# Loading the first MLP weight earlier, routing two steps per call, and turning the last layer's first group in slots 2 and 3

## The chip, the cores and the metric

The kernel runs on one core of a Trainium2 chip. The metric is the time of one execution on the device in microseconds (us), the median of several runs; lower is better. One execution is also recorded by the hardware profiler, and all rows in this document come from such records. Their engines are PE (TensorE matmuls), PEld (TensorE weight loads), DVE (VectorE), ACT (ScalarE), POOL (GpSimd) and SP (the sync engine, which here only issues DMAs; its queue is written SPq).

## The reference

Three layers follow each other: block-causal attention, a mixture of experts with one expert per token, and an MLP. Cut to what is computed:

```python
# attention: q, k, v are (4, 8, 576, 64) float32
scores = where(block_i >= block_j, q @ k.T / 8, -1e9)      # blocks of 64 tokens
attn = exp(scores - max); attn /= sum + 1e-9
x = (attn @ v) as (2304, 512)

# mixture of experts, 8 experts, 512 -> 1024 -> 512
logits = x @ w_gate + modality_bias[modality_id]
e_idx = argmax(logits); gate_w = softmax(logits)[e_idx]
for e in range(8):
    mask = e_idx == e
    out[mask] = gate_w[mask] * (maximum(x[mask] @ w1[e], 0) @ w2[e])

# MLP 512 -> 2048 -> 512; w_in and w_out arrive as float64
h = out @ w_in
g = where(h >= 1, h, where(h <= -1, 0, (h + 1)**2 / 4))
return g @ w_out
```

## The kernel before

The order of the work on each engine is written out by hand: within a stage every engine runs its instructions in the order in which the Python code emits them, and waits at an instruction until its operands and its buffer are there. Nothing overtakes on an engine, and nothing overtakes in SP's queue of DMA issues. A tile with a tag and a number of buffers reuses them in turn; the next user waits until the last reader is done.

The **slots** are the middle stage. Tokens are sorted by expert and cut into slots of 512 tokens; five slots (0 to 4) always run, the last with 384 tokens, and a branch behind them runs more where the routing asks for it. A slot has eight blocks `(s, f)`, one for 128 of the 1024 hidden columns. In a block, `first(s, f)` is 12 matmuls (w1 of the block times the slot's tokens, in three products of high and low parts) into a PSUM tile `h`; ACT makes `hh` of it and DVE `hl` (lines 1088 and 1089). `second` of the block before is 12 matmuls (9 in slot 4) into the accumulators `acc`. The weights come as `raw` tiles from SP (lines 539 and 541, four buffers); ACT makes the high part `wh` (line 1072) two blocks ahead and DVE the low part `wl` (line 1075) one block ahead. In blocks 3 to 6 `turn` transposes 128 tokens of the next slot on PE into a PSUM tile `xt` (line 1065), from which ACT makes `xhi` (line 75) and DVE `xlo` (line 76). That tile has the tag `tr` in the pool `pst`, which holds one buffer. At a slot's end `acc` is copied to `y` (lines 1105 and 1107) and scattered to `y_dram` by DMAs that POOL issues (line 1109).

`between(s, f, at)` is called four times in a block (`at` 0 to 3), and the side work hangs on it:

- The **routing** is a generator (`group`, `other_slots`) of small steps, mostly one to three DVE instructions. A call takes one step where `at` is even and two where it is odd, six in a block. Three of its steps use PE: the ranks `rkp` (lines 647 to 652), the inverse permutation `inv` (lines 696 and 697), and the tables `tabs` (line 912). Each puts its result in a tile of the same tag `tr`. Between the operands of `inv` and `inv` itself stand 12 steps that do nothing.
- **w_in** comes in 16 pieces of 512 KB (`load_wi`). SP issues the DMA of a piece (`wi_raw`, line 964, two buffers); then `cut_f64` lets 2 steps go by and makes float32 of float64: ACT squares (`sqi`, line 952), DVE does four operations (lines 954, 956, 958, 959). Last come the high part on ACT (line 969) and the low part, a subtraction on POOL (line 970). A step is taken in the calls with odd `at`, two in a block, by each of the last three pieces begun. Pieces are begun after the blocks from (2, 1) to (4, 4), 16 in 21 blocks.
- **The last layer's first group**: three tiles of 128 tokens are fetched from `y_dram` (`yr`, line 1016), scaled by the gate on DVE (line 1023) and transposed by `turn_y` (PE line 1031, ACT line 75, DVE line 76). `AHEAD` names the blocks of fetch, scale and turn for each of the three; all are in slot 4.

After slot 4 all engines pass the branch, and the last layer begins with `first` of its group 0 (line 991, `h<-yhi,wi`).

Of the kernel before, what the change touches and what calls it, by code (L numbers as in the profile page):

```python
# [11 lines left out]
F32 = mybir.dt.float32  # L12
# [6 lines left out]
ALU = mybir.AluOpType  # L19
# [17 lines left out]
NF, NF2 = F // P, F2 // P  # L37
# [5 lines left out]
NSTAT = 5  # L43
# [23 lines left out]
NG = G3 // P  # L67


AHEAD = ((4, 1), (4, 3), (4, 4)), ((4, 1), (4, 4), (4, 5)), ((4, 2), (4, 5), (4, 6))  # L70


def split_hi_lo(nc, hi, lo, src):
# [472 lines left out]
class Routing:  # L546
# [222 lines left out]
    def other_slots(self, ps):  # L769

        nc, V, t = self.nc, self.nc.vector, self.t
# [3 lines left out]
        def T(shape, dt, nm):  # L775
            return t.late_pool.tile(shape, dt, name=nm)
# [34 lines left out]
        nc.scalar.activation(ohp, oha, AF.Copy, scale=self.pcol)  # L811
        V.tensor_tensor(ohj, oha, self.tile0.to_broadcast([P, NJ, NS2]), op=ALU.mult)
        yield
        for _ in range(12):
            yield
        yield from self.inverse(ps("inv")[:, :NS2], U * NFIRST, NJ, ohp, ohj)
        yield "rows"
# [38 lines left out]
        more, some, few = T([P, 1, E], F32, "more"), T([P, 1], F32, "some"), T([P, 1], F32, "few")  # L856
# [20 lines left out]
        n, js, parts = NSORT, slice(0, NSORT), 5  # L877
# [18 lines left out]
                        op=ALU.is_equal)  # L896
# [29 lines left out]
def experts_and_mlp(ctx, bctx, late, tc, a_tail, weights, w_in, w_out, x_dram, y_dram, g_dram, out,  # L926
                    ident, half, tabs):
    nc = tc.nc
# [13 lines left out]
    def cut_f64(pool, u, raw, nm, wait, bufs=2):  # L942

        w = raw.bitcast(I32).rearrange("p (f w) -> p f w", w=2)
        top, bot = w[:, :, 1], w[:, :, 0]
        sq = pool.tile([P, 512], F32, tag="sq", name=f"sq{nm}", bufs=bufs)
        ti, ui = sq.bitcast(I32), u.bitcast(I32)


        for _ in range(wait):  # L950
            yield
        nc.scalar.activation(sq, top.bitcast(F32), AF.Square)
        yield
        nc.vector.scalar_tensor_tensor(sq, sq, 2.0 ** -30, top.bitcast(F32), op0=ALU.is_ge, op1=ALU.mult)

        nc.vector.tensor_scalar(ui, ti, 3, 0x3FFFFFFF, op0=ALU.logical_shift_left, op1=ALU.bitwise_and)
        yield
        nc.vector.scalar_tensor_tensor(ui, ti, -0x40000000, ui, op0=ALU.bitwise_and, op1=ALU.bitwise_or)
        nc.vector.scalar_tensor_tensor(ui, bot, 29, ui, op0=ALU.logical_shift_right, op1=ALU.bitwise_or)
        yield  # L960

    def load_wi(g):
        raw = tabs.cv.tile([P, 512], I64, tag="raw64", name=f"wi_raw{g}")
        nc.sync.dma_start(out=raw.rearrange("p (c f) -> p c f", f=P),
                          in_=w_in[:, g * P:(g + 1) * P].rearrange("(c p) f -> p c f", p=P))
        u = tabs.cv.tile([P, 512], F32, tag="cu", name=f"cui{g}", bufs=2)
        yield from cut_f64(tabs.cv, u, raw, f"i{g}", 2)
        hi, lo = (x.rearrange("p c f -> p (c f)") for x in wi[g])
        nc.scalar.copy(hi, u)
        nc.gpsimd.tensor_tensor(lo, u, hi.bitcast(F32), op=ALU.subtract)  # L970

    wo_raw, wo_left = {}, [z + i * NF2 // 2 for z in range(NF2 // 2) for i in range(2)]

# [26 lines left out]
    def open_right():  # L1000
        late.close()
        tabs.cv = pool("cv", 2, bctx)
        right = dict(side="right")
        res = pool("c_w", 1, **right)
        tabs.res = res

        for i, (tag, n, bufs) in enumerate(AREA):
            a = res.tile([P, n, 2, ND, P], F32R, tag=tag, name=f"wi{i}", bufs=bufs)
            wi.extend((a[:, z, 0], a[:, z, 1]) for z in range(n))
        tabs.rows = pool("c_rows", 3, yctx, **right)  # L1010
        y_ps.append(pool("c_y", 1, yctx, **right))
# [23 lines left out]


    def run_slots(slots, begin, between, part=0):
        blocks = [(s, f) for s in slots for f in range(NF)]

# [81 lines left out]
        for z, (s, f) in enumerate(blocks):  # L1121
            nxt = s + 1 if s + 1 in slots else None
            if f == 1 and nxt:
                gather(nxt)
            if z + CONV < len(blocks):
                convert(*blocks[z + CONV], 0)
            between(s, f, 0)
            if z + CONV - 1 < len(blocks):
                convert(*blocks[z + CONV - 1], 1)
            weights.load()  # L1130
            between(s, f, 1)
            if (s, f) == (NSTAT - 1, NF - 2) and not part:
                tc.mark_branch_hint_location("more", engines=ENGINES)

            first(s, f)
            between(s, f, 2)
            if z > 0:
                second(*blocks[z - 1])
            if f in TURNS and nxt:
                turn(nxt, TURNS.index(f))  # L1140
            between(s, f, 3)
# [27 lines left out]
    more = itertools.chain(early, routing.other_slots(lambda nm: pst.tile([P, 512], F32, tag="tr", name=nm)))  # L1169
    begun, conv = [], []  # L1170
    state = dict(more=True, placed=False)

    def between(s, f, at):
        last = at == 3
        if state["more"] and (s or f or last):
            for _ in range(1 + at % 2):
                try:
                    got = next(more)
                    if got == "experts":
                        for x in range(NFIRST, NSTAT):  # L1180
                            weights.know(x)
                            weights.blocks += [(x, f) for f in range(NF)]
                    elif got == "rows":
                        state["placed"] = True
                except StopIteration:
                    state["more"] = False
                    open_right()
                    break
        if at % 2:
            for x in conv:  # L1190
                next(x, None)
        if not last or s == 0:
            return
        assert state["placed"]
        for t, places in enumerate(AHEAD):
            for place, do in zip(places, (fetch, scale, turn_y)):
                if place == (s, f):
                    do(0, t)

        z, n, m = NF * (s - 2) + f + 1, NF2, NF * (NSTAT - 2) - 3  # L1200
        if z > 0 and z * n // m > (z - 1) * n // m and len(begun) < n:
            g = len(begun)
            begun.append(load_wi(g))
            conv[:] = begun[-3:]
# [329 lines left out]
```

## Time and profile before

| | |
|---|---|
| median of 3 runs | 853.55 us (853.25 to 854.59) |
| the profiled execution's own time | 853.72 us |
| its span, first to last instruction | 851.9 us |
| PE busy | 824.9 us (97%) |
| DVE, ACT, POOL busy | 604.9, 480.1, 226.0 us |
| slots 0 to 4 | 222.7 to 455.2 us of the span |

The page divides the span into 40 slices of 21.3 us and gives the busy tenths of each engine:

```
PE   6999999998999999999888999999999999999998
DVE  5778878789755564888774666666635788777774
```

(PE's row is the page's; a slice that reads 8 has up to 4 us without a matmul.) The slices that read 888 in PE's row are 405 to 469 us: slot 4 and the start of the last layer.

### The profile page before, as it was taken

The page shows a single profiled execution, that of the slowest core. Times are in us where ns is not written, and L with a number is a line of the kernel's source. Part 1 is how long each engine was busy: PE and PEld are TensorE (multiplying, and loading weights), DVE is VectorE, ACT ScalarE, POOL GpSimd, SP SyncE. Part 2 cuts the span into 40 slices and gives each one's busy share as a digit, 9 for nine tenths or more (in the row PEclk, how much of TensorE's full clock was granted, in tenths as well). Part 3 has the DMA queues.
Part 4 walks back from the last instruction along what each step waited for, and adds up shares of the span by engine and source line. Part 5 has one row for each costly group of instructions (what it writes and reads, how often), then busy time and mean ns, then how long its engine had stood idle before and what let it go on. Part 6 is the DMA issues. An engine that isn't in the chain of part 4 may idle for free. (4 is left out here: it accounts for less than half of the span.)

```text
span 851.9 us, 14940 instructions
## 1 busy us (share of the span) xinstructions
PE 824.9 (97%) x5430; PEld 738.9 (87%) x5430; DVE 604.9 (71%) x1098; ACT 480.1 (56%) x958; POOL 226.0 (27%) x265
## 2 busy tenths in 40 slices
PE   6999999998999999999888999999999999999998
PEld 5787787785888888888767999999999999999998
DVE  5778878789755564888774666666635788777774
ACT  5898888885534343445434666666656533343431
POOL 8555555556302212242312000110000012111110
PEclk8999999999999999999999999999999999999999
DMA  6343443430924445564642553554633454333301
GB/s 147 73 100 86 105 111 93 112 88 28 293 88 161 149 136 180 173 218 152 208 127 95 166 180 126 173 179 143 210 131 139 140 218 154 124 137 124 124 29 35
DMA packets 137294, 116.16 MB, mean 136 GB/s; under 512 B 69799, under 2 KB 122039, under 8 KB 134912
## 3 DMA queue, kind: packets, MB, share of 16 engines
q1 hardware_dynamic: 131488, 100.90, 38.6%
q0 software_dynamic: 4384, 13.92, 4.6%
q8 instruction: 44, 0.72, 0.4%
q10 hardware_dynamic: 1344, 0.33, 0.2%
q14 instruction: 34, 0.28, 0.1%
HBM read 82.09 MB, written 33.29 MB: 135 GB/s over the span
## 5 line engine op out<-in xcount | busy, mean ns | idle before, releaser
L991 PE MATMUL h<-yhi,wi 128*128 128x384 f32 x768 | 200.4, 338 | 1.1 <-ACTq L1225 1.1
L991 PEld LDWEIGHTS h<-yhi,wi 128*128 128x128 f32 x768 | 139.5, 188 | 1.6 <-ACTq L1225 1.6
L991 PE MATMUL h<-ylo,wi 128*128 128x384 f32 x384 | 129.2, 336 | 0.0
L325 ACT ACTIVATE pall<-s,nmax 128x384 f32<-128x384 f32 (+2 forms) x144 | 79.5, 559 | 26.7 <-DVE nmax L319 17.0
L1264 ACT ACTIVATE cl<-h,half 128x384 f32<-128x384 f32 x96 | 55.8, 581 | 68.5 <-PE h L991 61.2
L1268 DVE SCALAR_TENSOR_TENSOR gg<-cl,h 128x384 f32<-128x384 f32 x96 | 52.1, 551 | 49.0 <-ACT cl L1265 40.0
L1388 PE MATMUL p<-wo,s 128*128 128x256 f32 x648 | 83.6, 282 | 0.4 <-DVE rest L1407 0.4
L1388 PEld LDWEIGHTS p<-wo,s 128*128 128x128 f32 x648 | 80.3, 188 | 0.6 <-issue 0.6
L1432 POOL DMA_INDIRECT out_dram<-rest,tab x16 | 24.7, 1544 | 195.3 <-DVE rest L1415 168.7
L991 PEld LDWEIGHTS h<-ylo,wi 128*128 128x128 f32 x384 | 72.1, 188 | 0.0
L343 PE MATMUL pt<-ident,pall 128*128 128x128 f32 x400 | 64.7, 279 | 3.3 <-DVE pT L484 2.4
L991 PE MATMUL h<-xhi,wl 128*128 128x512 f32 (+2 forms) x164 | 61.9, 378 | 2.0 <-DVE wl L1075 1.9
L991 PE MATMUL h<-xhi,wh 128*128 128x512 f32 (+2 forms) x164 | 63.4, 386 | 0.0
L1100 PE MATMUL acc<-wh,hh 128*128 128x512 f32 x152 | 60.1, 396 | 3.2 <-ACT hh L1088 3.2
L1388 PE MATMUL p<-wo,a 128*128 128x256 f32 x486 | 62.7, 282 | 0.0
L1100 PE MATMUL acc<-wh,hl 128*128 128x512 f32 x152 | 60.1, 395 | 1.7 <-DVE hl L1089 1.7
L991 PE MATMUL h<-xlo,wh 128*128 128x512 f32 (+2 forms) x164 | 61.5, 375 | 0.0
L1388 PEld LDWEIGHTS p<-wo,a 128*128 128x128 f32 x486 | 60.3, 188 | 0.0
L1089 DVE SCALAR_TENSOR_TENSOR hl<-h,hh 128x512 fp32r<-128x512 f32 (+1 forms) x40 | 26.5, 662 | 47.5 <-ACT hh L1088 47.2
L1100 PE MATMUL acc<-wl,hh 128*128 128x512 f32 x152 | 59.7, 393 | 0.0
L368 PE MATMUL px<-pT,v 128*64 128x512 f32 (+4 forms) x320 | 52.4, 432 | 0.0
L1265 ACT ACTIVATE cl<-cl 128x384 f32<-128x384 f32 x96 | 50.5, 526 | 3.0
(314 smaller groups left out, 1830.5 us busy)
## 6 DMA issues: line engine op xcount, KB each, us to landing
raw<-in_moe_w_dram SPq DMA_DIRECT2D x80, 256.0 KB, 3.0
g_dram<-gg SPq DMA_DIRECT2D x48, 384.0 KB, 2.8
g<-g_dram SPq DMA_DIRECT2D x18, 1024.0 KB, 4.8
wi_raw<-in_moe_w_in_dram SPq DMA_DIRECT2D x16, 512.0 KB, 5.2
wo_raw<-in_moe_w_out_dram SPq DMA_DIRECT2D x16, 512.0 KB, 4.2
yr<-y_dram SPq DMA_DIRECT2D x18, 256.0 KB, 3.7
x_dram<-xrow SPq DMA_DIRECT2D x33, 128.0 KB, 1.8
v<-in_v_dram SPq DMA_DIRECT2D x32, 128.0 KB, 2.6
```

The lines of the kernel that those rows point to most:

```text
L325: nc.scalar.activation(pall[n % 2][:, o:o + w], pss[:, u:u + w], AF.Exp, bias=nm[:, x:x + 1], scale=1.0, accum_out=ssum[:, b, c, x:x + 1])
L343: nc.tensor.transpose(pt[:, kk, :], pa[:, o + kk * P:o + (kk + 1) * P], ident)
L368: nc.tensor.matmul(pxs[n][h * 64:(h + 1) * 64, s0 - 64:], io_t[n, "v"][:, kk, h * D:(h + 1) * D], pTs[n][:, kk, h, s0:], start=(kk == 0), ...
L991: nc.tensor.matmul(ps, a[za], b[zb], start=(i == 0), stop=(i == n - 1))
L1089: nc.vector.scalar_tensor_tensor(hl, ph, 0.0, hh.bitcast(F32), op0=ALU.max, op1=ALU.subtract)
L1100: nc.tensor.matmul(accs[s][u], a[:, us], b[:, 1, :], start=(f == 0 and i == 0), stop=(f == NF - 1 and i == 2))
L1264: nc.scalar.activation(cl, ph, AF.Relu, bias=half, scale=0.5)
L1265: nc.scalar.activation(cl, cl, AF.Square)
L1268: nc.vector.scalar_tensor_tensor(gg[:, :, f % 2, :], cl.rearrange(t3, t=P), 1.0, ph.rearrange(t3, t=P), op0=ALU.min, op1=ALU.max)
L1388: nc.tensor.matmul(accs[i], t[:, hl, z, :], w[:, wl], start=(z == 0 and x == 0), stop=(z == NZ - 1 and x == 2))
L1432: outs.append(nc.gpsimd.indirect_dma_start(out=out[:, :], out_offset=bass.IndirectOffsetOnAxis(ap=tabs.tab[:, j, 0:1].bitcast(U32), axis=0 ...
```

## The change

Four edits, which hang together through the order on the engines:

1. `between` takes two routing steps in every call, eight in a block, and the gap ahead of `inv` is 8 empty steps instead of 12. The routing ends in slot 1's block 5 instead of slot 2's block 1.
2. Pieces of w_in are begun from block (1, 6) on, 16 in 21 blocks to (4, 2), where no routing is left.
3. A piece waits 3 steps between its DMA and the square instead of 2, and its low part is made on DVE instead of POOL.
4. The last layer's first group is fetched after blocks (2, 2) and (2, 3), scaled after (2, 5) to (2, 7), and turned after (3, 0) to (3, 2).

```diff
-AHEAD = ((4, 1), (4, 3), (4, 4)), ((4, 1), (4, 4), (4, 5)), ((4, 2), (4, 5), (4, 6))
+AHEAD = ((2, 2), (2, 5), (3, 0)), ((2, 2), (2, 6), (3, 1)), ((2, 3), (2, 7), (3, 2))
...
-        for _ in range(12):
+        for _ in range(8):
             yield
         yield from self.inverse(ps("inv")[:, :NS2], U * NFIRST, NJ, ohp, ohj)
...
-        yield from cut_f64(tabs.cv, u, raw, f"i{g}", 2)
+        yield from cut_f64(tabs.cv, u, raw, f"i{g}", 3)
         hi, lo = (x.rearrange("p c f -> p (c f)") for x in wi[g])
         nc.scalar.copy(hi, u)
-        nc.gpsimd.tensor_tensor(lo, u, hi.bitcast(F32), op=ALU.subtract)
+        nc.vector.tensor_tensor(lo, u, hi.bitcast(F32), op=ALU.subtract)
...
-            for _ in range(1 + at % 2):
+            for _ in range(2):
...
-        if not last or s == 0:
+        if not last or state["more"]:
             return
...
-        z, n, m = NF * (s - 2) + f + 1, NF2, NF * (NSTAT - 2) - 3
+        z, n, m = NF * (s - 1) + f - 4, NF2, NF * (NSTAT - 1) - 10
         if z > 0 and z * n // m > (z - 1) * n // m and len(begun) < n:
```

What moves on the engines is shown at three places. First PE where `inv` stands (`xt1_1` is the turn of slot 1's second tile). Before, it follows a block's `first`:

```order
L991 MATMUL h0_7_3646<-xhi0_3174,wh0_7_3546 128x512
L991 MATMUL h0_7_3646<-xlo0_3175,wh0_7_3546 128x512
L991 MATMUL h0_7_3646<-xhi0_3174,wl0_7_3547 128x512
L696 LDWEIGHTS ohb_1301
L696 MATMUL inv_3663<-ohp_3556,ohb_1301 128x48
```

Now it follows a turn:

```order
L1100 MATMUL acc0_3_3353<-wl0_3_3322,hh0_3_3456 128x512
L1100 MATMUL acc0_3_3353<-wh0_3_3321,hl0_3_3457 128x512
L1065 MATMUL xt1_1_3546<-ident_65,xg1_1_3315 128x128 x4
L696 LDWEIGHTS ohb_1301
L696 MATMUL inv_3560<-ohp_3509,ohb_1301 128x48
```

`inv` moves from slot 0's block 7 to the end of its block 4, directly behind `xt1_1`, which has the same tag `tr`. The second place is PE where `tabs` stands. Before, it follows slot 1's last `second`:

```order
L1100 MATMUL acc1_3_3832<-wh1_7_4005,hh1_7_4127 128x512
L1100 MATMUL acc1_3_3832<-wl1_7_4006,hh1_7_4127 128x512
L1100 MATMUL acc1_3_3832<-wh1_7_4005,hl1_7_4128 128x512
L912 LDWEIGHTS ohb2_4032
L912 MATMUL tabs_4203<-rhs_4001,ohb2_4032 128x80
```

Now it follows the turn of slot 2's first tile:

```order
L1100 MATMUL acc1_3_3870<-wl1_2_3758,hh1_2_3910 128x512
L1100 MATMUL acc1_3_3870<-wh1_2_3757,hl1_2_3911 128x512
L1065 MATMUL xt2_0_3974<-ident_65,xg2_0_3826 128x128 x4
L912 LDWEIGHTS ohb2_3884
L912 MATMUL tabs_3989<-rhs_3844,ohb2_3884 128x80
```

`tabs` moves from the start of slot 2 to slot 1's block 3, and it too stands directly behind a tile of its own tag. The third place is DVE in slot 4, from `hl4_4` to `hl4_6` (`hl4_4` is the low part of block 4's `h`, `wl4_6` the low weight of block 6, the numbers behind `sqi` and `cui` those of the pieces). Before:

```order
L1089 SCALAR_TENSOR_TENSOR hl4_5_5267<-h4_5_5253,hh4_5_5266 128x384
L954 SCALAR_TENSOR_TENSOR sqi14_5201<-sqi14_5201,wi_raw14_5198 128x512
L956 TENSOR_SCALAR cui14_5200<-sqi14_5201 128x512
L76 TENSOR_TENSOR ylo0_5233<-yt0_1_5283,yhi0_5232 128x4x128
L1023 TENSOR_SCALAR yr0_2_5151<-yr0_2_5151,tab_75 128x512
L1075 TENSOR_TENSOR wl4_7_5243<-raw4_7_5114,wh4_7_5242 128x1024
L958 SCALAR_TENSOR_TENSOR cui14_5200<-sqi14_5201,cui14_5200 128x512
L959 SCALAR_TENSOR_TENSOR cui14_5200<-wi_raw14_5198,cui14_5200 128x512
L1089 SCALAR_TENSOR_TENSOR hl4_6_5313<-h4_6_5299,hh4_6_5312 128x384
```

Now:

```order
L1089 SCALAR_TENSOR_TENSOR hl4_5_5293<-h4_5_5279,hh4_5_5292 128x384
L958 SCALAR_TENSOR_TENSOR cui15_5203<-sqi15_5204,cui15_5203 128x512
L959 SCALAR_TENSOR_TENSOR cui15_5203<-wi_raw15_5201,cui15_5203 128x512
L1075 TENSOR_TENSOR wl4_7_5272<-raw4_7_5159,wh4_7_5271 128x1024
L970 TENSOR_TENSOR wi8_4047<-cui15_5203,wi8_4047 128x512
L1089 SCALAR_TENSOR_TENSOR hl4_6_5328<-h4_6_5314,hh4_6_5327 128x384
```

`ylo` and the scaling of `yr` are gone from slot 4, the low part of a piece (line 970) has come to DVE, and the last piece ends a block and a half earlier.

## Rows read from the trace of the kernel before

**Rows 1.** Windows: us, busy us of each engine (instructions), clock, DMA share, GB/s
```profile
230.00:412.00 182.00, 182.00 (x888) 150.83 (x887) 119.28 (x230) 74.43 (x109) 40.04 (x34) 1.00 0.50 160
412.00:455.20 43.20, 35.51 (x164) 28.72 (x163) 33.87 (x47) 17.81 (x30) 15.10 (x12) 0.96 0.44 137
455.20:470.00 14.80, 12.76 (x72) 12.44 (x72) 4.93 (x10) 7.33 (x14) 3.43 (x5) 1.00 0.52 160
```
**Rows 2.** Waits, 405 to 475 us, PE: us in total, times, longest
```profile
PE acc L1100 <- ACT hh L1088: 3.2, 2, 2.8
PE h L991 <- DVE wl L1075: 1.9, 2, 1.7
PE acc L1100 <- DVE hl L1089: 1.7, 1, 1.7
PE h L991 <- ACTq L1225: 1.1, 1, 1.1
PE yt L1031 <- POOL yr L1023: 0.9, 1, 0.9
PE yt L1031 <- DVE yr L1023: 0.8, 1, 0.8
```
**Rows 3.** Waits, 405 to 456 us, ACT and DVE
```profile
ACT sqi L952 <- DMA wi_raw<-in_moe_w_in_dram: 14.9, 5, 5.0
...
DVE hl L1089 <- ACT hh L1088: 11.3, 3, 6.1
```
**Rows 4.** Timeline, PE in slot 4: start, us, what, [idle before <-releaser]
```profile
422.94 0.44 PE L991 MATMUL h<-xhi,wl 128*128 128x384 f32 x1 [1.70 <-DVE wl L1075]
...
431.90 0.80 PE L1100 MATMUL acc<-wh,hh 128*128 128x512 f32 x1 [2.77 <-ACT hh L1088]
```
**Rows 5.** Windows of 2 us, columns as in rows 1
```profile
422.00:424.00 2.00, 1.06 (x6) 1.07 (x7) 1.97 (x3) 0.00 (x0) 0.00 (x0) 1.00 0.23 55
...
432.00:434.00 2.00, 2.00 (x5) 1.61 (x6) 1.89 (x5) 1.84 (x3) 0.00 (x0) 0.50 0.02 7
```
**Rows 6.** Timeline, ACT in slot 4
```profile
430.81 0.66 ACT L952 ACTIVATE sqi<-wi_raw 128x512 f32<-128x512 f32 x1 [4.98 <-DMA wi_raw<-in_moe_w_in_dram]
```
**Rows 7.** The tile `wi_raw`, its DMAs
```profile
DMA to landing us min/median/max: 3.6/5.2/7.3
```
**Rows 8.** Timeline, DVE around the start of slot 4, one operation behind another
```profile
408.17 0.68 DVE L954 SCALAR_TENSOR_TENSOR sqi<-sqi,wi_raw 128x512 f32<-128x512 f32 x1
408.96 0.43 DVE L956 TENSOR_SCALAR cui<-sqi 128x512 int32<-128x512 int32 x1
409.30 1.22 DVE L1075 TENSOR_TENSOR wl<-raw,wh 128x1024 fp32r<-128x1024 f32 x1
410.44 0.69 DVE L958 SCALAR_TENSOR_TENSOR cui<-sqi,cui 128x512 int32<-128x512 int32 x1
411.15 0.69 DVE L959 SCALAR_TENSOR_TENSOR cui<-wi_raw,cui 128x512 int32<-128x512 int32 x1
411.91 0.56 DVE L1089 SCALAR_TENSOR_TENSOR hl<-h,hh 128x384 fp32r<-128x384 f32 x1
412.38 1.28 DVE L1107 COPY y<-acc 128x512 f32<-128x512 f32 x2
```
**Rows 9.** Lines, DVE, 403.5 to 453.3 us: count, busy us, mean ns
```profile
L76 DVE TENSOR_TENSOR ylo<-yt,yhi 128x512 fp32r<-128x512 f32 x3 | 2.0, 676 | 0.0
L1023 DVE TENSOR_SCALAR yr<-yr,tab 128x512 f32<-128x512 f32 x3 | 1.4, 473 | 0.0
```
**Rows 10.** Timeline, a turn in slot 0: PE, ACT, DVE
```profile
262.77 0.60 PE L1065 MATMUL xt<-ident,xg 128*128 128x128 f32 x4
263.12 0.48 PE L991 MATMUL h<-xhi,wh 128*128 128x512 f32 x1
...
263.40 0.59 ACT L75 CAST xhi<-xt 128x512 fp32r<-128x512 f32 x1 [2.50 <-PE xt L1065]
...
264.02 0.69 DVE L76 TENSOR_TENSOR xlo<-xt,xhi 128x512 fp32r<-128x512 f32 x1 [2.40 <-ACT xhi L75]
```

## The prediction

> **What bounds the kernel now.** I read the windows of busy time by stage first, then PE's waits, then what ACT and DVE wait for in the stage that PE's waits lie in, and last the timeline there. Busy PE alone says little, as matmuls overlap, but idle PE is a loss. From 230 to 412 us PE is busy 182.00 of 182.00 us [rows 1]: in slots 0 to 3 nothing that ACT, DVE or a DMA saves is worth anything, and any wait put into PE's order there costs its whole length. Slot 4 is different. From 412 to 455.2 us PE is busy 35.51 of 43.20 us, so 7.69 us are idle, and the granted clock is 0.96 of the full one, which loses another 4% of 35.5 or 1.4 us [rows 1]. Together 9.1 us are to be had there, and little elsewhere near the change: the wait at the branch (1.1) and the first wait for `yr` in the last layer (0.9) [rows 2] are left alone.
>
> PE's waits in slot 4 are for `hh` (3.2), `wl` (1.9), `hl` (1.7) and the scaled `yr` (0.8) [rows 2], in sum 7.6, so they are the 7.69. None of their makers is slow; they stand in line. ACT waits 14.9 us in five places for a piece of w_in to land, and DVE 11.3 us for `hh` [rows 3]. The worst is at 430.81: the square starts after a wait of 4.98 us for its DMA [rows 6], `hh` is queued behind it, and PE stands 2.77 us [rows 4]. [...] A piece lands in 5.2 us in the middle, 7.3 at worst [rows 7], and before the square follows the DMA's issue by one block, in slot 4 PE's (35.5 - 1.4) / 8 = 4.3 us: too little.
>
> **The pieces of w_in in slot 4.** In the changed order only pieces 13 to 15 are loaded in slot 4, the square stands a block and a half behind the issue (6.4 us against 5.2), and on ACT it stands behind `hh` of its block, not ahead of it, so that a wait has most of a block before the next `hh` is due. Where a piece is begun two blocks after the one that holds its buffer (pieces 12 and 15), its DMA waits half a block for DVE's last read, and one block is left: ACT waits about 1 us there, which that slack hides. The fetches of `yr`, which stood in SP's queue between the weights and the pieces, are gone from slot 4 as well.
>
> DVE must keep pace too. From one start to the next, its operations take [rows 8]: 0.79 (line 954), 0.34 (956), 1.14 (`wl`), 0.71 (958), 0.76 (959), 0.47 (`hl`), and 1.28 for two copies. The subtraction that comes from POOL has no row on DVE. The nearest are `wl`, the same operation on twice the columns (1.14, half of it 0.57), and `xlo`, of the same size but from PSUM (0.69 busy) [rows 10]; I take 0.6. From the end of slot 3 to the end of slot 4 DVE then has 8 `hl`, 7 `wl`, two copies, 5 of lines 954 and 956, 6 of 958 and 959, and 6 subtractions: 3.8 + 8.0 + 1.3 + 5.7 + 8.8 + 3.6 = 31.2 us, against PE's 34.1. It loses three `ylo` and three scalings, 2.0 + 1.4 us busy [rows 9]. It fits, but blocks 4 and 5 carry 0.47 + 1.14 + 0.6 + 1.13 + 1.47 = 4.8 us each against PE's 4.3, after block 2, which has only 2.2. So `wl` of blocks 6 and 7 and `hl` of 5 may come late by half a microsecond. I leave 0.7 us of waits, between 0 and 4.0; the upper end is that pieces 13 and 14 land in 7.3 us, and each 2.1 us more is then handed on through `hi`, `hl` and `second`. Slot 4 gives back 9.1 - 0.7 = 8.4 us.
>
> **The subtraction in slots 2 and 3.** Ten of the sixteen run there, 6 us of DVE work. Over slots 0 to 3 DVE is busy 119.28 of 182 us [rows 1], and `hl` is needed only after the next block's `first`; that work hides it, so I cost it at nothing. Without that cover it would be up to 6 us, and less than nothing can't come of it where PE has no idle time.
>
> **The first group's fetch, scale and turn.** The three turns' transposes take 3 x 0.35 us of PE (262.77 to 263.12 in [rows 10]) in slot 3 instead of slot 4: no sum. The fetches go into SP's queue after block (2, 2), behind the scatter of slot 1's last tokens, which lies in block (2, 0), two blocks earlier; the weights queued behind them are needed three blocks later. Nothing.
>
> **Two routing steps per call.** The DVE work is the same and hidden as before, but PE's order is not. `inv` now stands directly behind the turn `xt1_1`, and `tabs` behind `xt2_0`, and both write the one buffer of tag `tr`. So PE must wait at each until ACT has made `xhi` and DVE `xlo` of the turned tile; `first` of the next block is queued behind. What that takes, a turn in slot 0 shows [rows 10]: the transposes start at 262.77 and PE goes on at 263.12, while `xlo` ends at 264.02 + 0.69 = 264.71. PE would have stood 1.6 us. Before, `inv` and `tabs` came a `first` or more after the last turn and waited for none of this. Each wait is at least `xhi` and `xlo` less the transposes' tail, 0.59 + 0.69 - 0.25 = 1.0, and at most 1.6 plus one `wl` ahead of `xlo` on DVE, 2.7; I take 1.6, since DVE has nothing else due there. Two make 3.2 us, between 2.0 and 5.4. The shorter gap ahead of `inv` (8 empty steps at two per call, four calls) still covers its operands, as `xlo` is later than they are. `rkp` also moves a block forward, to just behind the operation that makes its operand: 0 to one `wl` (1.1), which I take as 0, since that chain of small operations begins a block earlier.
>
> **The sum**, against the profiled execution's own 853.72 us (span 851.9, and 0.2 above the median of 853.55): -8.4 + 3.2 = -5.2, or 848.5 us.
>
> [...] In the trace a wait of 1.70 us left the clock at 1.00 [rows 4, 5], and only the one of 2.77 was followed by 0.50. [...]
>
> **The rivals.** *Late pieces:* 13 and 14 land as late as the worst before, and 4.0 us of waits stay in slot 4 instead of 0.7: 851.8. For it speaks that slot 3's scatters go out at the same time as piece 13; against it that fewer DMAs are queued than before. *The clock falls* at both new waits, at the 1.4 us that it cost once in slot 4 [rows 1]: 851.3. *The new waits don't show*, because PE finds the tile free or has slack behind them: 845.3; the order on PE speaks against it. *Slower: DVE stops at the subtraction.* On POOL the subtraction held up nothing. On DVE it waits for the high part on ACT (line 969), which is queued behind the next piece's square, and `hl` and `wl` are queued behind it. If ACT still stands at the squares of slot 4 for some 5 us, as at 430.81 [rows 6], all of DVE stands there too, and slot 4 keeps its 9.1 us. With the two new waits that is 853.7 + 3.2 = 856.9. It decides from about 3 us of wait at a square on, since `hl` has some 3.6 us between `hh` and its use (PE's 4.3 less `hh` and `hl`). Against it speaks the half block more that each DMA has.
>
> **How the numbers follow.** Forecast 0.54, late pieces 0.17, clock 0.06, hidden waits 0.10, DVE stopped 0.13. A measurement of this kernel can tell a difference of about 0.2%, 1.7 us, so faster means under 852.0. The forecast is faster but for 0.02; hidden waits always; late pieces, at 851.8, in half; the clock in 0.04; which makes 0.75. Slower, over 855.4, takes most of the last case, 0.11, and 0.14 is left between. The range runs from 844.5 (hidden waits, and slot 4 clean) to 853.0 (late pieces with longer new waits) and leaves out most of the slower case.
>
> **What would show it.** In the changed profile: PE idle under 1 us in slot 4 and its clock at 1.00; two PE waits of about 1.6 us on DVE's `xlo`, before `inv` and `tabs`, and no others from 230 us to slot 4; ACT's waits at the squares short or harmless. It is wrong if `hl` or `wl` still stop PE in slot 4 by more than 2 us, if DVE waits there for line 969, or if PE waits in slots 2 and 3.

## The result and the profile after

The changed kernel takes 846.71 us (846.23 to 846.87, 4 runs) against 853.48 us of the kernel before: a ratio of 0.9917, 95% interval 0.99 to 0.9934. On another chip, later, it was 0.991 (0.9894 to 0.9925). That is faster by 6.8 us; the prediction said 5.0 (848.5), with a range from 844.5 to 853.0. The profiled execution spans 844.9 us, 7.0 less than before. One of the six executions of `sub_pool2`, an experiment below, took 3317.88 us and stands outside its ratio.

First the windows by stage, which answer to [rows 1]; the last is slot 4 to the branch.

```profile
230.00:412.00 182.00, 179.20 (x880) 148.41 (x879) 124.78 (x249) 77.69 (x112) 25.96 (x25) 1.00 0.53 167
412.00:457.00 45.00, 43.46 (x218) 38.52 (x217) 28.23 (x43) 18.42 (x31) 7.85 (x7) 1.00 0.40 130
```
```profile
410.39:449.08 38.69, 37.15 (x181) 32.20 (x180) 29.55 (x45) 17.62 (x28) 6.19 (x6) 1.00 0.37 121
```

From 230 to 412 us PE, never idle before, has 2.80 us without a matmul; around slot 4 the idle time shrinks from 7.69 to 1.54, most of it the wait at the branch (1.1), which lies in this window and did not in that of before, and the clock is 1.00. PE's waits from 225 to 480 us (total, times, longest) say what the 2.80 are:

```profile
PE inv L696 <- DVE xlo L76: 1.4, 1, 1.4
PE tabs L912 <- DVE xlo L76: 1.4, 1, 1.4
PE yt L1031 <- POOL yr L1023: 1.2, 1, 1.2
PE h L991 <- ACTq L1225: 1.1, 1, 1.1
PE h L991 <- DVE wl L1075: 0.4, 2, 0.2
```

The waits for `hh`, `hl` and DVE's `yr` of [rows 2] are gone, the wait for `wl` is down from 1.9 to 0.4 us, and the two new ones are those that the prediction named. At the first of them PE's timeline shows the turn and then `inv`, behind a wait:

```profile
250.66 0.60 PE L1065 MATMUL xt<-ident,xg 128*128 128x128 f32 x4
252.66 0.18 PE L696 MATMUL inv<-ohp,ohb 128*128 128x48 bf16 x1 [1.40 <-DVE xlo L76]
```

In slot 4 (410.39 to 449.08 us) ACT and DVE wait as follows, against 14.9 and 11.3 us in [rows 3]:

```profile
ACT sqi L952 <- DMA wi_raw<-in_moe_w_in_dram: 5.1, 2, 2.7
...
DVE wi L970 <- ACT wi L969: 2.3, 2, 1.8
DVE hl L1089 <- ACT hh L1088: 1.8, 2, 1.6
```

An idle row says how long an engine stood, not what the end was delayed by. For that the starts of the same matmul in both traces are subtracted. Time between the first matmuls of blocks (us):

| from, to | before | after | difference |
|---|---|---|---|
| first of the slots, slot 1 block 0 (`inv` lies in it) | 47.06 | 48.57 | +1.51 |
| slot 1 block 0, slot 2 block 2 (`tabs`) | 57.01 | 58.53 | +1.52 |
| slot 2 block 2, slot 4 block 0 (three turns come in) | 79.52 | 80.91 | +1.39 |
| slot 4 block 0, first of the last layer (three turns go) | 50.06 | 38.69 | -11.37 |
| first of the last layer, the `first` behind the first `yt` | 14.12 | 14.35 | +0.23 |
| from there to the first `p` of the last product | 195.47 | 195.47 | 0.00 |

The slots also began 0.28 us earlier (222.38 instead of 222.66), in work that the change doesn't touch. The sum is -7.0, the difference of the spans. Without the turns, slot 4 gave back 11.37 - 1.39 = 9.98 us and the two waits took 3.03.

### The profile page after: what moved, and what is told of

Same layout as the page of the kernel before. It is cut to its first block, busy times and chain, and to the rows that moved or that the text cites. A ratio compares the mean times of both kernels' runs of the same rounds, so it can differ in the third digit from the quotient of the medians.

```text
span 844.9 us, 14924 instructions
## 1 busy us (share of the span) xinstructions
PE 822.9 (97%) x5430; PEld 738.8 (87%) x5430; DVE 605.8 (72%) x1114; ACT 480.9 (57%) x958; POOL 201.6 (24%) x249
## 4 chain that ended last, share of the span: by engine, by line
PE 68%; DVE 9%; issue 8%; DMA 7%; ACT 6%; POOL 2%; POOLq 0%; SPq 0%; ACTq 0%; DVEq 0%
PE h L991 27%; PE p L1388 20%; PE acc L1100 6%; DMA y_dram<-y,sidx 6%; PE pt L343 3%; PE px L368 3%; ACT pall L325 2%; PE xr L420 2%; PE s L291 1%; ACT qa L234 1%; DVE nmax L319 1%; PE s L302 1%; DVE nmax L323 1%; DVE kd L272 1%; PE s L301 1%
## 5 line engine op out<-in xcount | busy, mean ns | idle before, releaser
L1072 ACT CAST wh<-raw 128x1024 fp32r<-128x1024 f32 x40 | 41.9, 1051 | 18.8 <-PE acc L1100 18.7
```

The lines of the kernel that those rows point to most:

```text
L1072: nc.scalar.copy(ws[s, f][0], weights.raw[s, f])
```

## Experiments

The runs were made on several chips, on which the kernel before took 853.1 to 856.6 us; each time below is compared with the kernel before on its own chip. Terms under 2 us are read from the starts of blocks: up to slot 4 these agree between two executions of the same kernel to 0.03 us (from the first matmul of the slots to slot 4's first: 188.01 and 188.02 us in the changed kernel, 187.98 and 188.00 in `sub_pool` and `sub_pool2`, 184.94 and 184.95 in `free` and `free2`). Slot 4 itself varies more: 38.69 and 37.63 us in the changed kernel.

### What the routing edit costs

`route_only`, on the kernel before:

```diff
-        for _ in range(12):
+        for _ in range(8):
...
-            for _ in range(1 + at % 2):
+            for _ in range(2):
```

> The kernel before with only the first edit: two routing steps in every call and 8 empty steps ahead of inv; pieces of w_in, the subtraction and the first group as they were. Theory: the two new waits on xlo, ahead of inv and tabs, are the price of this edit and nothing else in it counts; by the changed kernel's starts of blocks (first matmul of block 0 to that of slot 1: +1.51 us over before; over tabs +1.52) the time rises by 3.0 us, from 853.5 to 856.5 (856.0 to 857.0). Rival: the waits are swallowed in slot 4, where PE waited for other things in the kernel before anyway, and the time stays at 853.5. Second rival: the stall in slot 4 moves with them and the clock falls at another place, 1.5 us either way: 855 or 858.

Measured: 859.82 against 856.55 us, ratio 1.0045 (1.0031 to 1.0058). By block starts the slots are 3.02 us longer up to slot 4's first matmul, as expected, but slot 4 itself takes 48.52 instead of 50.06 us, and PE waits 0.6 us more for the last layer's first `yr`: 2.0 us up to the first `p`. The theory holds for the two waits; half of their price was swallowed in this execution by stalls that fell otherwise, so part of the first rival is true. Between the 2.0 us of the record and the 3.3 of the medians the runs don't decide.

`tile_h`, on the changed kernel, puts `inv` and `tabs` (and the ranks `rkp`, which come from the same generator) into the tag `h`, which has three buffers, and leaves the order alone; `tile_h_gap5` also lets two more empty steps go by ahead of `tabs`:

```diff
-    more = itertools.chain(early, routing.other_slots(lambda nm: pst.tile([P, 512], F32, tag="tr", name=nm)))
+    more = itertools.chain(early, routing.other_slots(lambda nm: psh.tile([P, 512], F32, tag="h", name=nm)))
```
```diff
-        for _ in range(3):
+        for _ in range(5):
             yield
         tp = ps("tabs")[:, :parts * n]
```

> The changed kernel with inv and tabs in a tile of tag h (three buffers) instead of tr (one buffer); the order of all instructions is the same. Theory: the wait ahead of inv is for the buffer alone. Its operands are ready when the turn ends (ohj ends at 250.67 us, the turn's transposes at about 251.2), so 1.5 us go. Ahead of tabs there is a second reason behind the first: the last part of ohb stands on DVE behind xlo (294.58 + 0.28 = 294.86 us), so only some 0.2 us go there. Together 1.7: 846.7 to 845.0. Rival: both waits are for the buffer, 3.0 us go: 843.7. Second rival: inv and tabs wait for something of the turn that is not the buffer, nothing goes: 846.7.

> The kernel tile_h with 5 empty steps ahead of tabs instead of 3, so that tabs follows the first of slot 1's block 4 and not the turn xt2_0. Theory: by then xlo and the last part of ohb are done, and the second new wait goes as well: 1.5 us less than the changed kernel for inv and 1.5 for tabs, 846.7 to 843.7 (843.3 to 844.1), with no wait of PE from 230 us to slot 4. Rival: the later reading of tabs by DVE, which now stands behind hl, delays the end of the routing and with it the pieces of w_in, and PE waits in slot 4 again: 845 or more.

Measured: `tile_h` 847.27, `tile_h_gap5` 847.07, the kernel before 856.55 us there; ratios 0.9899 (0.9884 to 0.9914) and 0.9889 (0.9874 to 0.9905). What PE still waits for in `tile_h` from 225 to 480 us:

```profile
PE yt L1031 <- POOL yr L1023: 1.4, 1, 1.4
PE h L991 <- ACTq L1225: 1.1, 1, 1.1
PE tabs L912 <- DVE ohb L906: 1.1, 1, 1.1
PE h L991 <- DVE wl L1075: 0.2, 1, 0.2
```

With another buffer and the same order, the wait ahead of `inv` is gone (1.55 us by block starts). That ahead of `tabs` only changed its releaser, from `xlo` to the last `ohb` that stands behind `xlo` on DVE, and gave 0.35 us. The two empty steps took away the rest: 1.51 us at `tabs`. The medians do not show these last 1.2 us (847.27 and 847.07): in the recorded executions the slots begin at 224.81 us in `tile_h` and at 226.56 in `tile_h_gap5`, a difference that arises ahead of them. The finding rests on the starts of blocks and on PE's waits. So `inv` waited for the buffer alone, and `tabs` for the buffer and, behind it, for an operand. The rivals fall.

### What gave slot 4 its time back

Three kernels undo parts of the change, all else as changed: `ahead_s4` has the old `AHEAD`; `wait2` has two steps ahead of the square; `late2` has these two steps and begins the pieces as before.

```diff
-AHEAD = ((2, 2), (2, 5), (3, 0)), ((2, 2), (2, 6), (3, 1)), ((2, 3), (2, 7), (3, 2))
+AHEAD = ((4, 1), (4, 3), (4, 4)), ((4, 1), (4, 4), (4, 5)), ((4, 2), (4, 5), (4, 6))
```
```diff
-        yield from cut_f64(tabs.cv, u, raw, f"i{g}", 3)
+        yield from cut_f64(tabs.cv, u, raw, f"i{g}", 2)
```
```diff
-        z, n, m = NF * (s - 1) + f - 4, NF2, NF * (NSTAT - 1) - 10
+        z, n, m = NF * (s - 2) + f + 1, NF2, NF * (NSTAT - 2) - 3
```

> The changed kernel with 2 steps between a piece's DMA and its square instead of 3, as in the kernel before; all else as changed. Theory: the half block matters only where blocks are short. In slots 0 to 3 nothing shows (PE has no wait there). In slot 4 the square stands 4.2 us behind the issue, less than the 5.2 us of a landing, and again ahead of hh in its block; with three pieces there ACT waits 1 to 3 us and PE stands once or twice: 1 to 3 us of the 10 come back, so 4 to 6 us under the kernel before instead of 6.8. Rival: the half block is what did it, the stalls for hh come back whole, and the clock with them: 3 us over the kernel before. Second rival: with the yr fetches and the fourth piece gone from SP's queue the pieces land early enough; no change, 6.8 under.

> The changed kernel with the first group's fetch, scale and turn back in slot 4 (AHEAD as in the kernel before). Theory: the turns' 1.4 us of PE only change their place; but DVE gets 3.4 us more in slot 4 (three scalings, three ylo) beside the subtraction, where wl was already late by 0.4 us, and the turn waits for yr (0.8 before): 2 to 4 us come back, 3 to 5 under the kernel before. Rival: moving the group changes nothing, the pieces alone did it: 6.8 under. Second rival: the fetches in SP's queue are what made the pieces land late; with them back ACT waits at a square for 4 us or more, PE stands for hh and the time is that of the kernel before or above it.

> The changed kernel with the pieces begun as in the kernel before ((2, 1) to (4, 4)) and with 2 steps ahead of the square; the first group stays in slots 2 and 3, the subtraction on DVE, the routing at two steps per call. Theory: the pieces in slot 4 are what stops PE; 5 of the 10 us or more come back, 2 under to 3 over the kernel before. Rival: the first group's work in slot 4 was the cause; the time stays 5 to 7 under. Third: with the subtraction on DVE behind hi, the stop of all DVE that the prediction's slower case names: more than 3 over the kernel before.

Measured against 853.06 us: `wait2` 850.81 (0.9969, 0.9958 to 0.9981), `ahead_s4` 848.88 (0.9946, 0.9929 to 0.9963), `late2` 852.41 (0.9987, 0.9974 to 0.9999). The stage from slot 4's first matmul to the last layer's, one edit after the other:

| kernel | us | step |
|---|---|---|
| before | 50.06 | |
| `route_only` | 48.52 | -1.54, two routing steps per call |
| `late2` | 43.40 | -5.12, the first group out of slot 4 (1.39 of it the turns, which only move) and the subtraction on DVE, which no run separates |
| `wait2` | 41.48 | -1.92, pieces begun earlier |
| the changed kernel | 38.69 | -2.79, the square half a block later |

No edit alone did it: without the turns the three steps behind `route_only` are 3.7, 1.9 and 2.8 us. Each row is one record, and the two of the changed kernel differ by 1.06 us, so a step is uncertain by about as much. `late2` came out nearly as its theory had it (4.7 of the 10 us came back where 5 or more were expected, 0.7 under the kernel before); its third case, DVE stopped, did not come. `ahead_s4` did too (4.2 under, slot 4 1.8 us longer than in the changed kernel without the turns), though ACT's long wait at a square, which its second rival named, was there as well. Two rows side by side, from kernels that differ in `AHEAD` too, speak for the place of the square as what counts, and not ACT's wait as such. In `ahead_s4` ACT stood 4.58 us at a square, where the half block later puts `hh` ahead of it:

```profile
431.15 0.67 ACT L952 ACTIVATE sqi<-wi_raw 128x512 f32<-128x512 f32 x1 [4.58 <-DMA wi_raw<-in_moe_w_in_dram]
...
435.59 0.50 PE L1100 MATMUL acc<-wh,hl 128*128 128x512 f32 x1 [0.71 <-DVE hl L1089]
```

In `wait2` a shorter wait, with `hh` behind it, stopped PE for more than twice as long:

```profile
427.39 0.66 ACT L952 ACTIVATE sqi<-wi_raw 128x512 f32<-128x512 f32 x1 [3.99 <-DMA wi_raw<-in_moe_w_in_dram]
...
428.48 0.50 PE L1100 MATMUL acc<-wh,hh 128*128 128x512 f32 x1 [1.81 <-ACT hh L1088]
```

`wait2` came out slower than expected (2 us under the kernel before, not 4 to 6). The recorded execution, the slowest of twelve (849.42 to 852.69 us), shows a reason outside slot 4; whether it holds for the others isn't shown. In it the first `yt` of the last layer waited 2.10 us for `yr`, against 1.2 in the changed kernel, and the clock fell behind it, which took another 1.6 us (197.07 instead of 195.47 us from the next `first` to the first `p`). PE alone, in windows of 1 us (busy, clock, DMA share, GB/s):

```profile
467.00:468.00 1.00, 0.58 (x5) 1.00 0.92 350
468.00:469.00 1.00, 1.00 (x7) 0.82 0.97 373
469.00:470.00 1.00, 1.00 (x5) 0.50 1.12 413
470.00:471.00 1.00, 1.00 (x5) 0.50 0.98 391
471.00:472.00 1.00, 1.00 (x5) 0.50 0.94 333
472.00:473.00 1.00, 1.00 (x7) 0.98 0.08 27
```

### What the subtraction on DVE costs

`sub_pool` and, later, `sub_pool2` are the changed kernel with

```diff
-        nc.vector.tensor_tensor(lo, u, hi.bitcast(F32), op=ALU.subtract)
+        nc.gpsimd.tensor_tensor(lo, u, hi.bitcast(F32), op=ALU.subtract)
```

and `after_again` is the changed kernel itself, on the chip of `sub_pool2`.

> The changed kernel with the subtraction of the low part of w_in back on POOL. Theory: the engine of the subtraction does not matter, since neither DVE nor POOL is waited for there: 846.7, within 0.5 either way. Rival one: DVE's 0.6 us for each piece are what PE still waits for in slot 4 (0.4 us for wl): 846.3. Rival two: a subtraction on POOL slows DVE's operations beside it (line 956 took 1.33 instead of 0.43 us beside one in the kernel before), and wl or hl come late again in slot 4: 848 to 850.

> The changed kernel itself, unaltered, beside sub_pool2 and free2, since earlier runs were on different chips. By the starts of its blocks (226.7 us from the first matmul of the slots to the branch, 233.65 before) and 0.2 us more at the first yt: 6.8 us under the kernel before.

> The kernel sub_pool again, beside the changed kernel. Theory: the subtraction on DVE is what the 1.2 us left in slot 4 are (37.5 us from its first matmul to the branch with it on POOL, 38.7 with it on DVE): 1.2 us under after_again, 8.0 under the kernel before. Rival: the difference is chance between two executions: the same as after_again.

Measured: `sub_pool` 848.55 against 856.55 us (0.9903, 0.9888 to 0.9918). Its slot 4 took 37.51 us and not 38.69, so a cost of 1.2 us for the subtraction on DVE was the next theory. On one chip, against 854.13 us, `after_again` took 846.29 (0.991) and `sub_pool2` 845.72 (0.990, 0.9884 to 0.9916), and their slot 4 took 37.63 and 37.66 us: the theory falls as a fixed cost, and the rival (chance between two executions) holds. What differs between the two records of the same kernel can be read. In the first, ACT waited 2.72 us for a piece, the high part came late, DVE stood 1.84 us at the subtraction, and `hl` and `wl`, queued behind it, came late to PE:

```profile
430.29 0.68 ACT L952 ACTIVATE sqi<-wi_raw 128x512 f32<-128x512 f32 x1 [2.72 <-DMA wi_raw<-in_moe_w_in_dram]
...
432.46 0.69 DVE L970 TENSOR_TENSOR wi<-cui,wi 128x512 fp32r<-128x512 f32 x1 [1.84 <-ACT wi L969]
...
437.20 0.44 PE L991 MATMUL h<-xhi,wl 128*128 128x384 f32 x1 [0.24 <-DVE wl L1075]
```

In `after_again` the same piece had ACT wait 1.33 us, and DVE 0.46; PE did not wait at all:

```profile
429.90 0.70 ACT L952 ACTIVATE sqi<-wi_raw 128x512 f32<-128x512 f32 x1 [1.33 <-DMA wi_raw<-in_moe_w_in_dram]
...
432.09 0.69 DVE L970 TENSOR_TENSOR wi<-cui,wi 128x512 fp32r<-128x512 f32 x1 [0.46 <-ACT wi L969]
```

By starts, slot 4 of the first record lost the 1.1 us at three places, one `hl` and two `wl`, all behind that stop of DVE. So the mechanism of the prediction's slower rival exists, at a price of 0 to 1.1 us by the landing of one DMA, not of 8.

### A version that beats both

`free` and `free2` are `tile_h_gap5` with the subtraction on POOL.

> The kernel tile_h_gap5 (inv and tabs in tag h, 5 empty steps ahead of tabs) with the subtraction on POOL as in the kernel sub_pool. Theory: what each took away is a different wait (1.5 + 1.5 us at inv and tabs, 0.4 for tabs' place, 0.5 to 1.2 of wl, hl in slot 4), so they add: from the first matmul of the slots to the branch 222.8 us instead of 223.3 for tile_h_gap5, 225.5 for sub_pool and 226.7 for the changed kernel, and 10 us under the kernel before. Rival: the POOL subtraction's own slowing of DVE beside it takes it back, 223.5 or more.

> The kernel free again, beside the changed kernel. Theory: the two new waits (3.0 us) and the subtraction on DVE (1.2 us) add up: 4.2 us under after_again, 11.0 under the kernel before. Rival: what the waits ahead of the last layer's first yt give (1.4 instead of 1.2 us) takes some back: 3.5 under after_again.

Measured: `free` 843.25 against 853.06 us (0.9878, 0.9859 to 0.9897); `free2` 842.71 against 854.13 (0.9867, 0.9849 to 0.9886), all its runs (842.48 to 843.21) under all of `after_again` (845.32 to 846.95): 3.6 us. From the first matmul of the slots to the branch `free` took 222.43 us and `free2` 222.75, against 222.8 expected. What PE waits for from 225 to 480 us in `free2`:

```profile
PE yt L1031 <- POOL yr L1023: 1.2, 1, 1.2
PE h L991 <- ACTq L1225: 1.1, 1, 1.1
```

Of the 3.6 us, 3.0 are the two waits (225.65 to 222.75 us, `after_again` to `free2`, is 2.9). The subtraction has no share that shows, where 1.2 us were expected: slot 4 took 37.80 us in `free2` and 37.63 in `after_again`. Nor do the 0.6 us between the medians of `sub_pool2` and `after_again` come from there: from the first matmul of the slots to the branch the two took 225.66 and 225.65 us.

## Why the prediction was right, and where its sizes were off

**What bounds the kernel.** Right. PE had no slack from slot 0 to slot 3, and all that ACT, DVE or POOL did there cost nothing: ten subtractions on DVE, the first group's fetches, scalings and `ylo` showed no wait of PE from 230 us to slot 4 but the two foreseen.

**The new waits.** Right in place, releaser and size: 1.4 us of idle each and 1.51 and 1.52 by the starts of blocks, where 1.6 was said, from the one turn in [rows 10]. `tile_h` shows the shared buffer to be the reason at `inv`; at `tabs` the prediction missed that the last `ohb` stands behind `xlo` on DVE and would have held PE nearly as long.

**Slot 4.** This is the step whose size was off: "Slot 4 gives back 9.1 - 0.7 = 8.4 us" was 9.98 in the profiled execution and 50.06 - 37.63 - 1.39 = 11.04 in `after_again`. The clock's share was sized well: the nine matmuls that follow the stop of 2.77 us took 3.54 us from the first start to the turn behind them (431.90 to 435.44), the nine ahead of block 4's `first`, at a granted 1.00, 2.08 (424.78 to 426.86): 1.46, where 1.4 was said. What was too small is the idle time, taken as 7.69 from [rows 1]. An idle row counts from the modelled end of the last matmul, 0.33 us behind its start, where the next would have started 0.17 us behind it. The starts around the wait for `wl` in the kernel before show it:

```profile
420.73 0.33 PE L991 MATMUL h<-xhi,wh 128*128 128x384 f32 x1
420.90 0.34 PE L991 MATMUL h<-xlo,wh 128*128 128x384 f32 x1
...
423.22 0.34 PE L991 MATMUL h<-xhi,wh 128*128 128x384 f32 x1
423.39 0.34 PE L991 MATMUL h<-xlo,wh 128*128 128x384 f32 x1
```

From 420.90 to 422.94 [rows 4] are 2.04 us where 0.17 is the pace, 1.87 lost for a wait listed as 1.70, and the first matmul behind it has 0.28 us to the next start instead of 0.17. This stop so cost 0.28 us more than its row. Slot 4 had six (0.17, 0.40, 1.70, 2.77, 0.82 and 1.68 us, in sum 7.5), which by the starts around them lost 8.9 us, and two of 0.06 us for `wl` (at 441.11 and 447.07), too short for the list, which lost 0.33 each. With the clock's 1.46 that is 11.1 us. What was to be had in slot 4 is 50.06 - 37.49 - 1.39 = 11.2 us, with `free` as the stage without a stop, so what the idle rows leave out makes up the difference from 9.1. The residual of 0.7 was 1.2 in the profiled execution and 0.1 in `after_again`. That the yr fetches, the later square and fewer pieces all count was right in kind; the prediction gave them no shares, and the runs did, to about a microsecond and in the one order that they were undone in.

**What it left at nothing.** The first `yr` of the last layer's second group: 0.9 to 1.2 us in the profiled execution, 0.5 to 2.1 in the others.

"On POOL the subtraction held up nothing" and "None of their makers is slow" were misread. In slot 4 of the kernel before, line 956 took 1.33 us three times (at 437.59, 443.55 and 449.51) instead of 0.43, each time while POOL ran line 970:

```profile
443.11 1.49 POOL L970 TENSOR_TENSOR wi<-cui,wi 128x512 fp32r<-128x512 f32 x1 [4.47 <-ACT wi L969]
443.55 1.33 DVE L956 TENSOR_SCALAR cui<-sqi 128x512 int32<-128x512 int32 x1
```

From 431.88 to 453.24 us DVE ran there without a pause, and PE's waits for `yr` (0.82) and `hl` (1.68) are for operations of that stretch. By the rows the three held DVE up by 3 x 0.90 = 2.7 us; how much of this reached PE is not shown, since no run moves the subtraction alone in the kernel before.

**The rivals.** Late pieces came in half a dose: ACT waited 2.4 and 2.7 us at the squares of pieces 13 and 14, where the prediction had no wait, but PE only 0.4 by its rows and 1.2 by starts. The clock did not fall at the new waits: they took 1.40 us each, and the windows of 1 us around both show 1.00. That it might fall there was the author's supposition from the one fall in the kernel before, behind a wait of 2.77 us. That the new waits would not show was wrong. The slower one had its mechanism right (line 970 behind 969 behind a late square): DVE's wait for line 969 in slot 4, 2.3 us in the changed kernel, was even named as a sign that the forecast is wrong, and came. Its price was wrong: it was said to decide from 3 us of ACT's wait on (its slack of 3.6 us is 3.4 by the 4.3 less 0.47 each for `hh` and `hl`) and to keep slot 4's 9.1 us, but in `ahead_s4`, where ACT waited 4.6 us and DVE 3.3, slot 4 took 41.85 us, with the turns, against 50.06. DVE had worked ahead, and most of its stop ran beside matmuls whose operands were already there: the stop ended at 433.31 us, and PE's first wait behind it is the 0.71 at 435.59.

**The sum.** Slot 4 -9.98 instead of -8.4, waits +3.03 instead of +3.2, the second group's `yr` +0.23 and the start of the slots -0.28 instead of nothing: -7.0 instead of -5.2.

## What to carry to other kernels

Before an instruction is moved to another place on a full engine, look up what shares its output buffer there: here a gain of 10 us paid 3 us for two small products that came to stand behind another user of a one-buffer tag, and a tag with free buffers, with two empty steps ahead of one of them, gave it back. Size a stop by the starts on both sides of it against the usual pace, not by its idle row, and compare each row of an engine with others of its kind before it is called not slow. And where an operation waits for a DMA, what counted here was which urgent instruction stood behind it on its engine, more than how long it waited.

## What the runs showed of the hardware

Which stops of PE were followed by the lower clock (granted 0.50 instead of 1.00). From the slots on, behind waits of 1.40 (twice, the changed kernel), 1.66 (`route_only`), 1.68 and 1.70 (before) and 1.81 us (`wait2`) the windows show 1.00 throughout; behind waits of 1.91 (`late2`), 2.10 (`wait2`), 2.27 (`route_only`) and 2.77 us (before) they show about three us at 0.50, at a price of 1.46 us in the kernel before and 1.6 us in `wait2`. `route_only` behind its wait of 2.27 us:

```profile
428.00:429.00 1.00, 0.00 (x0) 1.00 0.00 0
429.00:430.00 1.00, 0.36 (x2) 1.00 0.48 147
430.00:431.00 1.00, 1.00 (x7) 0.80 0.99 367
431.00:432.00 1.00, 1.00 (x5) 0.50 0.68 167
432.00:433.00 1.00, 1.00 (x4) 0.50 0.74 241
433.00:434.00 1.00, 1.00 (x4) 0.50 0.97 327
```

From the slots on each of the four falls followed a single stop, and the two short new waits, 42 us apart, were followed by no fall. Just ahead of the slots it is otherwise: in the records of `route_only`, `sub_pool` and `tile_h_gap5` a stop of 1.3 us and, after 0.8 us of matmuls, one of 1.51 were followed by 3.4 us at 0.50, though neither is as long as the 1.81 that passed elsewhere. So in these records the length of a single stop alone does not decide. `route_only` there, PE:

```profile
216.57 0.33 PE L343 MATMUL pt<-ident,pall 128*128 128x128 f32 x1 [1.35 <-issue]
216.73 0.66 PE L420 MATMUL xr<-rh,xT 128*128 128x144 f32 x4
218.90 1.46 PE L343 MATMUL pt<-ident,pall 128*128 128x128 f32 x6 [1.51 <-DVE pT L484]
```
```profile
219.00:220.00 1.00, 1.00 (x6) 0.50 1.11 360
```

In `tile_h`, with a stop of 1.32 us at the same place and one of 0.99 behind it, the windows show 1.00.

Slower rows of line 956 beside POOL's line 970 cost nothing in `free2`: two of its five in slot 4 took 1.39 and 1.33 us instead of 0.43, and PE did not wait there.
